# A transformer block on one core: another order of its pieces, three first loads through the Activation queue, multiplications by zero at the beginning, the last tile stored by halves

## The chip, the core and the metric

The kernel runs on one core of a Trainium2 chip. A core has a matrix engine (PE in the profile, with its weight loads shown as PEld), a vector engine (DVE), a scalar or activation engine (ACT), a general engine (POOL) and a synchronising engine (SP) that mostly issues DMA transfers. Each engine works through its own queue of instructions strictly in the order in which they were written and waits on semaphores for the others. The metric is the time of one launch in microseconds, as the device measures it; lower is better. The change is judged by the median of the runs.

## What is computed

One block of a transformer, all in float32: 2048 tokens of width 512, attention with 32 heads of width 16 in a sliding window of 256 tokens, and a gated feed-forward part of width 1376.

```python
h  = x + attention(layernorm(x), wqkv) @ wo      # causal, i - j < 256, softmax
g  = layernorm(h) @ w_gate                       # 512 x 1376
u  = layernorm(h) @ w_up                         # 512 x 1376
h2 = h + (sigmoid(g) * u) @ w_down               # 1376 x 512
```

## The kernel before

**Arithmetic.** Every float32 operand is split into a high and a low half of 16 bits, and a product is three matrix multiplications (high by high, high by low, low by high). So most of DVE's and ACT's work is to scale, to split (a cast for the high half, line 357 or 355, and a subtraction for the low one, line 362) and to take products out of PSUM. The weights need a scale first: the maximum of their absolute values (line 367 on ACT, line 369 on DVE), spread over the partitions by a small multiplication with the identity (line 380, the function `scale`).

**Tiles and stages.** The tokens are eight blocks `b` of 256, or sixteen tiles `t` of 128. For each block: layer norm (lines 556 to 573), split, transposition (the first four tiles by PE, line 609, the others by a DMA), query and key products (line 402, taken out at 661), a regrouping of queries and keys by DMA into `SQ` and `SK`, scores for the row maximum (lines 740 and 725), scores again in the transposed form (lines 794 to 805), exponentials on ACT (770), masks on POOL (778, 783), the product with V (831, taken out at 843), the division (873, 875), split into `whl`, and the product with `wo` (402 again, taken out at 899). The queries of a block go to `SQ` in transfers of 128 KB (`SQ<-sq`), the keys through DRAM (`mem<-sk`, then `SK<-mem`, 384 KB each).

The feed-forward part works on pairs of tiles `p` (0 to 7). Gate and up products are done in seven products instead of eight on operands that were added up beforehand (line 1140; the operands made of the weights come from lines 1026 and 1045, those made of the tokens from line 1122), the hidden values are gated and split (1206 to 1224), transposed by DMA (1240), and multiplied with `w_down` (function `do_down`, lines 1317 and 1323), whose weights are split at 954 and 956. `do_down` keeps two PSUM banks, A and B, of 512 columns; every half of a bank is a sum over many multiplications, and DVE adds it to the residual at lines 1288 and 1300. A finished tile of 128 by 512 is stored by line 1294 (256 KB).

**What sets the order.** Each step is a generator that yields, before each piece, what the piece needs and which engine it goes to. A planner has written down in which order the pieces are emitted: the table `ORDER` (lines 61 to 283), one number for each piece, which names the step and, where a piece can be done by more than one engine (`alt`: a cast on ACT or DVE, a subtraction on DVE or POOL), also the engine. `Planner.run` (line 312) replays it. The emitted order is the order of every engine's queue. PSUM has rings: three banks for the row maxima, two for transposed scores, two for the other products, and a single one for the product with V, so line 843 must have taken out one product before the next may start.

**The queue of the transfers.** Before the change all transfers are issued by SP, in one order. A transfer from SP waits until the one that held its semaphore eight transfers earlier is complete, and for the engines that its row names; everything behind it on SP waits too.

Of the kernel before, what the change touches and what calls it, by code (L numbers as in the profile page):

```python
# [35 lines left out]
P = 128  # L36
# [246 lines left out]
]  # L283

class Port(float):
# [1214 lines left out]
```

## Time and profile before

| | |
|---|---|
| runs | 770.92, 771.59 and 772.53 us, median 771.59 us |
| profiled execution | 770.99 us, of which its span (first to last instruction) is 769.3 us |
| mean granted clock of PE | 0.989 |
| busy in the span | PE 729.6, DVE 692.9, ACT 436.9, POOL 256.7 us |
| transfers | 118.57 MB, 154 GB/s on average |

Busy time counts an instruction from its start to its modelled end. A multiplication's end lies in the next ones, so a PE that is shown busy may still have short gaps. In the table of waits, each row names the instruction that waited, what released it, the sum of the waits, their number and the longest. In the windows, each engine's busy time in a stretch stands beside the granted clock of PE (1.00 is full speed), the mean busy share of the sixteen DMA engines and the GB/s they moved. In the list by time, a row is one instruction or a run of equal ones: start, duration, engine, line, operation, output and input.

### The profile page before, as it was taken

Reading aid. Unit: us, or ns where it says so; the run is one execution under the profiler, and the core shown is the slowest. Engines: PE = TensorE matmul, PEld = TensorE weight load, DVE = VectorE, ACT = ScalarE, POOL = GpSimd, SP = SyncE. Lnnn points to the kernel's source line nnn. Section 1 sums busy time; section 2 is a strip of 40 time slices with the busy share of each in tenths; the row PEclk is TensorE's granted clock in tenths of the full one; section 3 lists DMA queues with packets and bytes.
Section 4 is the critical chain, followed back from the end, with each engine's and each line's share of the span. In section 5 each row is a group of like instructions: output and inputs, shape, how many; then the busy total and the mean of one; then the engine's idle time right before and its main releaser. Section 6 shows DMA issues by size and latency. Waiting matters only on the chain.

```text
span 769.3 us, 19057 instructions
## 1 busy us (share of the span) xinstructions
PE 729.6 (95%) x7030; PEld 502.0 (65%) x7030; DVE 692.9 (90%) x2067; ACT 436.9 (57%) x774; POOL 256.7 (33%) x319
## 2 busy tenths in 40 slices
PE   4899999999999999999999898699999999999997
PEld 3586678777686687686666554367565666666476
DVE  8999999978899999999998579999998989989973
ACT  5755788878688888798877667653222111121210
POOL 3333445535545466554757442240000000000000
PEclk9999999999999999999999999899999999999999
DMA  8586593886747989569587879455375665736535
GB/s 300 156 221 168 142 180 80 152 198 144 165 95 172 205 211 182 166 156 245 150 162 180 211 187 274 117 119 105 79 136 95 117 131 106 150 66 109 96 83 155
DMA packets 210318, 118.57 MB, mean 154 GB/s; under 512 B 174576, under 2 KB 183792, under 8 KB 210224
## 3 DMA queue, kind: packets, MB, share of 16 engines
q1 hardware_dynamic: 210224, 117.35, 67.9%
q8 instruction: 55, 0.90, 0.5%
q14 instruction: 39, 0.32, 0.2%
HBM read 43.65 MB, written 19.40 MB: 82 GB/s over the span
## 4 chain that ended last, share of the span: by engine, by line
PE 75%; DVE 11%; DMA 5%; issue 5%; ACT 3%; SPq 0%; DVEq 0%; ACTq 0%
PE mmp L402 18%; PE sp L1140 14%; PE mmp L1317 11%; PE pvp L831 7%; PE sp L740 6%; PE stp L1140 6%; PE pvp L1140 3%; PE stp L805 2%; PE stp L795 2%; DVE junk L725 2%; PE stp L794 1%; PE mmp L1323 1%; PE stp L796 1%; DMA oT<-whl 1%; ACT pa L770 1%
## 5 line engine op out<-in xcount | busy, mean ns | idle before, releaser
L725 DVE CUSTOM_DVE_ANT_0 junk<-sp,mask 128x320 uint8<-128x320 f32 (+4 forms) x512 | 215.4, 465 | 16.6 <-PE sp L740 14.0
L770 ACT ACTIVATE pa<-stp,kappa 128x512 f32<-128x512 f32 (+1 forms) x256 | 157.3, 645 | 48.0 <-PE stp L796 44.5
L1140 PEld LDWEIGHTS <-x 128*128 128x128 f16 x1008 | 98.3, 98 | 94.6 <-issue 10.1
L740 PE MATMUL sp<-SK,SQ 96*128 96x256 f16 (+3 forms) x960 | 129.6, 233 | 6.3 <-DVE mq L725 3.1
L402 PE MATMUL mmp<-xT,W 128*128 128x256 f16 x768 | 114.3, 281 | 3.3 <-DVE sq L661 1.7
L740 PEld LDWEIGHTS <-SQ 96*128 96x128 f16 x960 | 80.5, 97 | 30.9 <-issue 12.8
L1140 PE MATMUL sp<-W,x 128*128 128x512 f16 (+1 forms) x420 | 90.1, 351 | 6.5 <-ACT SQ L355 5.8
L770 ACT ACTIVATE pb<-stp,kappa 128x512 f32<-128x512 f32 x128 | 84.6, 685 | 19.7 <-PE stp L805 15.9
L402 PEld LDWEIGHTS <-W 128*128 128x128 f16 x768 | 71.4, 100 | 16.1 <-DVE W L539 2.9
L778 POOL TENSOR_SCALAR_AFFINE_SELECT pa<-pa 128x1024 f32<-128x1024 f32 x56 | 62.9, 1127 | 53.9 <-ACT pa L770 50.3
L831 PE MATMUL pvp<-pa,VT 128*17 128x128 f32 (+1 forms) x1408 | 62.5, 307 | 0.0
L795 PE MATMUL stp<-SQ,SK 100*128 100x256 f16 x224 | 60.2, 272 | 0.0
L563 POOL TENSOR_TENSOR rs<-rs,nhalf 128x1 f32<-128x1 f32 x32 | 20.2, 634 | 118.2 <-DVE rs L560 105.0
L783 POOL TENSOR_SCALAR_AFFINE_SELECT pa<-pa 128x512 f32<-128x512 f32 x64 | 42.6, 669 | 45.3 <-ACT pa L770 45.0
L1206 ACT ACTIVATE SQ<-sp,cg 128x512 f32<-128x512 f32 (+1 forms) x22 | 14.0, 636 | 76.6 <-PE sp L1140 76.3
L796 PE MATMUL stp<-SQ,SK 100*128 100x128 f16 x256 | 55.5, 219 | 0.7 <-ACT pb L770 0.4
L783 POOL TENSOR_SCALAR_AFFINE_SELECT pb<-pb 128x512 f32<-128x512 f32 x64 | 42.0, 658 | 42.6 <-ACT pb L770 40.1
L402 PE MATMUL mmp<-WO,oT 128*128 128x512 f16 x192 | 51.4, 389 | 2.5 <-DMA oT<-whl 2.5
L831 PEld LDWEIGHTS pvp<-pa,VT 128*17 128x17 f32 x1408 | 37.8, 97 | 22.7 <-issue 2.7
L362 DVE TENSOR_TENSOR SQ<-SQ,SQ 128x512 f16<-128x512 f32 (+3 forms) x93 | 50.2, 555 | 1.9 <-ACT SQ L355 1.3
L794 PE MATMUL stp<-SQ,SK 100*128 100x128 f16 x224 | 49.5, 221 | 1.3 <-DMA SQ<-mt 0.3
L805 PE MATMUL stp<-SQ,SK 100*128 100x256 f16 x256 | 48.1, 272 | 2.5 <-ACT pa L770 2.1
(226 smaller groups left out, 1445.8 us busy)
## 6 DMA issues: line engine op xcount, KB each, us to landing
SQ<-sq SPq DMA_DIRECT2D x96, 128.0 KB
wr<-chunk SPq DMA_DIRECT2D x28, 256.0 KB
SK<-mem SPq DMA_DIRECT2D x16, 384.0 KB
chunk<-in_wd_dram SPq DMA_DIRECT2D x20, 256.0 KB
X<-in_x_dram SPq DMA_DIRECT2D x16, 256.0 KB
mem<-sk SPq DMA_DIRECT2D x8, 512.0 KB
out_dram<-X SPq DMA_DIRECT2D x16, 256.0 KB
W<-wr SPq DMA_DIRECT2D x7, 512.0 KB
```

What stands on the lines that cost most here:

```text
L402: PE.matmul(ps, a_of(a, k), b_of(b, k), start=(k == 0 and i == 0), stop=(k == n - 1 and i == 2))
L725: V.tensor_tensor_reduce(out=junk[:, c0:], in0=ps[:, c0:], in1=mask[:, c0:], scale=1.0, scalar=-3.0e38, op0=ALU.add, op1=ALU.max, accum_ou ...
L740: PE.matmul(ps[:, col:col + k1 - k0], q, SK[0:96, (2 * a + hf) % 5, 4 * (p % 2) + j, k0:k1], start=True, stop=True)
L770: S.activation(dst, a, AF.Exp, scale=kappa)
L778: G.affine_select(out=f, in_=f, pattern=[[0, 8], [-1, 128]], compare_op=ALU.is_gt, fill=0.0, base=0, channel_multiplier=1)
L783: G.affine_select(out=p, in_=p, pattern=[[0, 4], [1, 128]], compare_op=ALU.is_ge, fill=0.0, base=0, channel_multiplier=-1)
L795: PE.matmul(a[:, 128:384], ks(k0 + 1, g, j), qs(b, g, j, 0, 256), start=True, stop=True)
L796: PE.matmul(a[:, 384:512], ks(k0 + 3, g, j), qs(b, g, j, 128, 256), start=True, stop=True)
L805: PE.matmul(a[:, u, :], ks(k0 + 2, g, j + u), qs(b, g, j + u, 0, 256), start=True, stop=True)
L831: PE.matmul(ps[32 * j:32 * j + 17, u, q0:q1], VT[:, kt % 6, 8 * j + g, :], w[:, j, c:c + q1 - q0], start=first, stop=last, skip_group_chec ...
L1140: PE.matmul(ps, X2[p % 2][part][:, (a * COUNT[part] + at) * 2 + k, :], operand(c, j)[:, b, k, :], start=first and k == 0 and i == 0, stop= ...
L1317: PE.matmul(ps, hT[p, c, r][:, a, half * kinds[c] + i, :], W["d"][2 * c + i][:, b, j, :], start=fresh and c == 0 and i == 0 and n == 0, st ...
```

## The change

Four things are changed; all else in the program is the same.

1. The table `ORDER` is replaced as a whole. Its first row, before and after:

```diff
-    3203, 3331, 771, 899, 1027, 1155, 7424, 2179, 2435, 7808, 7426, 1411, 7424, 641, 2051, 7810, 7424, 641, 1539, 7424, 1667, 7808, 641, 7427, 7808,
...
+    3331, 899, 3203, 771, 1027, 1155, 7808, 3587, 2179, 7424, 2691, 2051, 7426, 641, 1539, 7810, 7424, 641, 2435, 7424, 7424, 641, 1795, 7808, 7427,
```

2. Tile 1 of x and the second and fourth quarter of the query weights are loaded by ACT's queue instead of SP's.

3. PE multiplies zeros: fourteen multiplications of 512 columns before anything else, two more behind the first group of eight transpositions and four behind the second. The operand is the buffer `stage[1][0]`, which POOL sets to zero at the beginning anyway; the result goes to a bank of the transposed scores and is not read.

4. In the last pair of tiles the last group of multiplications on bank A is emitted in another order. The three short multiplications that finish its upper 256 columns stand ahead of the last 15 + 3 on the lower ones; DVE then adds the upper half to the residual (line 1337 of the new file) and it is stored (line 1338); the lower half follows alone.

```diff
+    unread, zero = psum_tile("st", [P, 512]), stage[1][0].rearrange("p h j i u t -> p (h j i u t)")
+    turns = [2, 4]
+
+    def warm(n):
+        for i in range(n):
+            PE.matmul(unread, zero[:, :P], zero[:, :512], start=True, stop=True)
+
+    warm(14)
...
-        nc.sync.dma_start(xs[t][0], x[t * P:(t + 1) * P, :])
+        (nc.scalar if t == 1 else nc.sync).dma_start(xs[t][0], x[t * P:(t + 1) * P, :])
...
-        nc.sync.dma_start(wsrc[nm][:, k, :], src[k * P:(k + 1) * P, :])
+        (nc.scalar if nm == "q" and k % 2 else nc.sync).dma_start(wsrc[nm][:, k, :], src[k * P:(k + 1) * P, :])
...
+            if turns:
+                warm(turns.pop(0))
...
+            cols = slice(0, HALF if t == NT - 1 else D)
+            nc.sync.dma_start(out[t * P:(t + 1) * P, cols], home(t)[:, cols])
...
+                if ahead and c == 0:
+                    assert ("h", p, 2, ahead[0]) in plan.done
+                    rest(which, *ahead)
+                    x = home(2 * p + 1)[:, HALF:]
+                    V.scalar_tensor_tensor(x, bank[which][:, HALF:], cd, x, op0=ALU.mult, op1=ALU.add)
+                    nc.sync.dma_start(out[(2 * p + 1) * P:(2 * p + 2) * P, HALF:], x)
...
+        upper = 1, HALF, HALF, False
+        last = p == NT // 2 - 1
+        e = yield from step("A", 0, 5, 1, 1, False, [("r7", p)], ((1, 0, 0, False), upper), upper if last else None)
+        plan.add(prio, taken("r4", "A", t2, 0, HALF if last else D, [e, ("r7", p)], 0))
```

`rest` is the old loop over the short multiplications, now a function. The new file is 9 lines longer from line 446 on and up to 25 lines longer further down; in the rows below, lines 482 and 496 are the loads (473 and 487 before), 854 is 843, 886 is 875, 736 is 725, 697 is 686, 937 is 926 and 688 is 677.

**The start of ACT's queue.** Before, the loading of the table of functions stands first, and then the maxima of the query weights `wq` (each waits for a DMA semaphore) and their scaled copies:

```order
L1496 UNCONDITIONAL_BRANCH [waits barrier_Pool_Activation_PE_DVE_SP_release]
L367 ACT_TABLE_LOAD
L367 ACTIVATE W1_87,am_121<-wq_117 128x512 [waits DMAHW2_49]
L367 ACTIVATE W1_87,am_121<-wq_117 128x512 [waits DMAHW3_49]
L367 ACTIVATE W1_87,am_121<-wq_117 128x512 [waits DMAHW4_49]
L367 ACTIVATE W1_87,am_121<-wq_117 128x512 [waits DMAHW5_49]
L537 ACTIVATE W1_87<-wq_117,sq_196 128x512 [waits DVE_49]
```

After:

```order
L1521 UNCONDITIONAL_BRANCH [waits barrier_Pool_Activation_PE_DVE_SP_release]
L482 DMA X_69<-in_x_dram 128x512
L496 DMA wq_132<-in_wqkv_dram 128x512 x2
L367 ACT_TABLE_LOAD
L367 ACTIVATE W1_87,am_136<-wq_132 128x512 [waits DMAHW3_49]
L367 ACTIVATE W1_87,am_136<-wq_132 128x512 [waits DMAHW2_49]
L367 ACTIVATE W1_87,am_136<-wq_132 128x512 [waits DMAHW5_49]
L367 ACTIVATE W1_87,am_136<-wq_132 128x512 [waits DMAHW4_49]
L546 ACTIVATE W1_87<-wq_132,sq_204 128x512 [waits DVE_49]
```

Three transfers now stand ahead of the table's loading, and SP's queue has three fewer ahead of its next ones.

**SP's queue around one of the `SK<-mem` loads** (the keys of a block for the row maxima; in the execution before it is issued at 227.73 us). Before, rows 179 to 184 of SP's queue:

```order
L854 DMA_TRANSPOSE RT_75<-RH_77 128x8x128 [waits DMAHW7_49,DVE_49]
L752 DMA_TRANSPOSE mt_4154<-mh1_114 128x1x128 [waits DMAHW0_49,DVE_49]
L926 DMA chunk_4163<-in_wd_dram 128x512 [waits DMAHW1_49]
L756 DMA SQ1_79<-mt_4154 2x32x64 [waits DMAHW2_49,DMAHW0_49]
L756 DMA SQ1_79<-mt_4154 2x32x64 [waits DMAHW3_49]
L677 DMA SK_78<-mem_2887 96x2048 [waits DMAHW4_49,PE_49]
```

After, rows 179 to 184:

```order
L865 DMA_TRANSPOSE RT_75<-RH_77 128x8x128 [waits DMAHW6_49,Activation_49]
L767 DMA SQ1_79<-mt_4167 2x32x64 [waits DMAHW7_49,DMAHW5_49]
L767 DMA SQ1_79<-mt_4167 2x32x64 [waits DMAHW0_49]
L937 DMA chunk_4205<-in_wd_dram 96x512 [waits DMAHW1_49]
L937 DMA chunk_4220<-in_wd_dram 128x512 [waits DMAHW2_49]
L688 DMA SK_78<-mem_2918 96x2048 [waits DMAHW3_49,PE_49]
```

Two loads of the down weights (192 and 256 KB) stand directly ahead of the keys, where before there was one, with two small transfers between.

**DVE's queue ahead of one taking-out of a product with V** (the 26th of 32; in the execution before it is at 377.56 us). `whl` is the split of the attention's output, `rc` its reciprocal, `mh` the row maxima on their way to the queries. Before:

```order
L873 RECIPROCAL rc_7362<-OS_76 128x32 [waits Pool_49]
L357 CAST whl_7368<-OS_76 128x512 [waits DMAHW3_49,Pool_49]
L747 TENSOR_SCALAR mh0_113<-mq_6907 128x32 [waits DVE_49]
L748 SCALAR_TENSOR_TENSOR mh0_113<-mq_6907,mh0_113 128x32 [waits DVE_49]
L899 SCALAR_TENSOR_TENSOR X_69<-mmp_6940,co_2867,X_69 128x512
L362 TENSOR_TENSOR whl_7368<-OS_76,whl_7368 128x512
L843 SCALAR_TENSOR_TENSOR RH_77<-pvp0_111,RH_77 128x2x256 [waits Activation_49]
```

After:

```order
L736 ISA junk_7367,mq_6916<-sp_7350,mask_124 128x320 [waits DVE_49,PE_49]
L736 ISA mq_6916 128x1
L886 TENSOR_TENSOR OS_76<-OS_76,rc_6899 128x32x16
L854 SCALAR_TENSOR_TENSOR RH_77<-pvp0_126,RH_77 128x2x256 [waits Activation_49]
L736 ISA junk_7397,mq_7321<-sp_7386,mask_124 128x320 [waits DVE_49,PE_49]
```

The cast and the subtraction of this `whl` are no longer on DVE (they are on ACT and POOL), the row maxima's and the residual's rows come later, and a multiplication by an earlier reciprocal stands there instead.

More of the change, by code (lines that the diff above doesn't have):

```diff
@@ L1293, in taken @@
             e, = yield {DMA_: 0.475}, [e] + needs[1:], [], 0.73
-            nc.sync.dma_start(out[t * P:(t + 1) * P, :], home(t))
+            cols = slice(0, HALF if t == NT - 1 else D)
+            nc.sync.dma_start(out[t * P:(t + 1) * P, cols], home(t)[:, cols])
             plan.mark(("out", t), e)
@@ L1301, in high, with rest, step @@
             plan.mark((key, p), e)
-        def step(which, lo, j, r, half, fresh, needs, extra=()):
+        def rest(which, row, col, at, over):
+            R = F - (NF - 1) * P
+            for n, (a, b) in enumerate(((0, 0), (0, 1), (1, 0))):
+                PE.matmul(bank[which][:, at:at + HALF], hT[p, 2, row][:R, a, 2, :], W["l"][:R, b, col:col + HALF], start=over and n == 0, stop=n == 2,
+                          skip_group_check=not over)
+        def step(which, lo, j, r, half, fresh, needs, extra=(), ahead=None):
             nonlocal places
@@ L1318, in step @@
                                   stop=c == 2 and n == 2, skip_group_check=not fresh)
-            for row, col, at, over in extra:
-                e, = yield {PE_: 0.3265}, [("h", p, 2, row), ("W", "d", len(PAIRS))]
-                R = F - (NF - 1) * P
-                for n, (a, b) in enumerate(((0, 0), (0, 1), (1, 0))):
-                    PE.matmul(bank[which][:, at:at + HALF], hT[p, 2, row][:R, a, 2, :], W["l"][:R, b, col:col + HALF], start=over and n == 0, stop=n == 2,
-                              skip_group_check=not over)
+            for piece in extra:
+                e, = yield {PE_: 0.3265}, [("h", p, 2, piece[0]), ("W", "d", len(PAIRS))]
+                if piece != ahead:
+                    rest(which, *piece)
             return e
@@ L1338, in do_down @@
         plan.add(prio, taken("r3", "B", t1, 0, D, [e, ("r6", p)], 1))
-        e = yield from step("A", 0, 5, 1, 1, False, [("r7", p)], ((1, 0, 0, False), (1, HALF, HALF, False)))
+        upper = 1, HALF, HALF, False
+        last = p == NT // 2 - 1
+        e = yield from step("A", 0, 5, 1, 1, False, [("r7", p)], ((1, 0, 0, False), upper), upper if last else None)
         plan.mark(("hTf", p), e)
-        plan.add(prio, taken("r4", "A", t2, 0, D, [e, ("r7", p)], 0))
+        plan.add(prio, taken("r4", "A", t2, 0, HALF if last else D, [e, ("r7", p)], 0))
     work = kappa = cg = cd = hl2 = ws = None
```

440 rows, old and new, of the table ORDER are left out of this document.

## The prediction

> **What bounds the kernel now.** I read the page's totals first, then PE's waits, then windows, since a total hides which engine sets the pace where.
>
> ```profile
> span 769.3 us, 19057 instructions
> ...
> PE 729.6 (95%) x7030; PEld 502.0 (65%) x7030; DVE 692.9 (90%) x2067; ACT 436.9 (57%) x774; POOL 256.7 (33%) x319
> ```
>
> PE and DVE are both near full; ACT and POOL are not. PE's waits:
>
> ```profile
> PE mmp L609 <- DVE RT L357: 7.0, 1, 7.0
> PE sp L1140 <- ACT SQ L355: 6.4, 2, 5.8
> PE sp L740 <- DVE mq L725: 3.1, 6, 1.2
> PE mmp L402 <- DVE sq L661: 1.7, 1, 1.7
> PE sp L380 <- POOL RT L362: 1.6, 1, 1.6
> PE sp L740 <- DMA SK<-mem: 1.6, 1, 1.6
> PE mmp L1317 <- DMA RH<-SQ: 0.8, 1, 0.8
> ```
>
> They are the beginning (7.0, 1.6), one wait of 5.8 and one of 1.6 for keys. The windows show who is full around them (busy us by engine, PE's granted clock, DMA share, GB/s):
>
> ```profile
> core 0: us, PE busy (x) PEld busy (x) DVE busy (x) ACT busy (x) POOL busy (x), PEclk, DMA share, GB/s
> 0.00:12.30 12.30, 2.83 (x18) 2.01 (x18) 9.07 (x22) 4.83 (x11) 5.34 (x13) 1.00 0.84 270
> 22.00:24.00 2.00, 0.28 (x2) 0.10 (x3) 1.94 (x4) 1.98 (x5) 0.00 (x0) 1.00 0.17 66
> 26.00:28.00 2.00, 2.00 (x11) 1.40 (x10) 1.87 (x7) 1.22 (x2) 0.00 (x0) 0.50 1.03 170
> 12.30:138.00 125.70, 117.80 (x1209) 88.29 (x1210) 120.78 (x466) 92.52 (x187) 51.48 (x67) 0.99 0.67 168
> 138.00:200.00 62.00, 62.00 (x805) 47.32 (x802) 53.91 (x202) 49.67 (x86) 31.96 (x42) 1.00 0.75 162
> 204.00:212.00 8.00, 6.32 (x102) 4.34 (x101) 5.84 (x19) 3.72 (x7) 3.75 (x6) 1.00 1.05 217
> 212.00:216.00 4.00, 4.00 (x30) 3.25 (x30) 2.98 (x13) 2.63 (x4) 0.00 (x0) 0.57 0.56 171
> 344.00:392.00 48.00, 47.05 (x585) 32.11 (x588) 46.31 (x155) 40.02 (x67) 25.97 (x31) 1.00 0.81 190
> 452.00:484.00 32.00, 29.50 (x193) 13.93 (x193) 30.62 (x62) 23.50 (x42) 9.99 (x9) 0.95 0.97 240
> 484.00:496.00 12.00, 4.90 (x30) 2.82 (x29) 11.97 (x22) 7.37 (x15) 2.00 (x2) 0.85 0.50 120
> 496.00:500.00 4.00, 3.84 (x19) 2.11 (x18) 4.00 (x10) 2.51 (x6) 0.79 (x1) 0.60 0.42 93
> ```
>
> To 138 us DVE sets the pace (120.78 of 125.70; at 22 to 24 PE idles, and has half its clock at 26 to 28), then PE (62.00 of 62.00); at 344 to 392 both are full; at 452 to 496 DVE (30.62 and 11.97 of 44) makes PE idle, and PE then runs at 0.60.
>
> **The beginning.** The rows on which it turns:
>
> ```profile
> 0.94 1.81 POOL L444 MEMSET sq<- 128x2048 f32 x1
> 1.72 1.85 SPq L487 DMA_DIRECT2D wq<-in_wqkv_dram  x4
> 6.97 1.33 PE L609 MATMUL mmp<-identh,RT 128*128 128x128 f16 x8 [6.97 <-DVE RT L357]
> 6.45 0.63 ACT L367 ACTIVATE W<-wq 128x512 f16<-128x512 f32 x1 [4.37 <-DMA wq<-in_wqkv_dram]
> 8.85 0.63 ACT L367 ACTIVATE W<-wq 128x512 f16<-128x512 f32 x1
> 9.60 0.16 DVE L531 TENSOR_REDUCE am<-am 128x1 f32<-128x4 f32 x1 [1.05 <-ACT W L367]
> 9.91 0.76 PE L380 MATMUL sp<-ident,am 128*128 128x128 f32 x2 [1.60 <-POOL RT L362]
> 13.16 5.24 PE L402 MATMUL mmp<-xT,W 128*128 128x256 f16 x25 [0.18 <-DVE W L539]
> 18.24 0.39 PE L380 MATMUL sp<-ident,am 128*128 128x128 f32 x2
> 18.47 2.46 PE L402 MATMUL mmp<-xT,W 128*128 128x256 f16 x21
> ```
>
> The four `wq` quarters took SP 1.85 us to issue; by two queues the six first loads are issued about three issue times (1.4 us) sooner. What that is worth is bounded by DVE, which waited only 1.05 us for the last maximum: its rows ahead of that are its own work. Beside it, the small multiplication of `scale` took 0.76 us on a slow PE and 0.39 later. So at most 1.05 + 0.37 = 1.4 us come off. ACT now issues three transfers (0.46 each, 1.85 / 4) before loading its table, 1.4 us later; it idled 4.37 us ahead of its first quarter, so this is hidden, and would cost up to 1.4 only if that quarter came 3 us sooner.
>
> The Trainium skill ("Trainium Kernel Development and Optimization", Key Constraints) says that issuing from several engines saves only issue time, since the same 16 DMA engines move the data. By that the term is the 1.4 us of issue at most; the DMA share of 0.84 in the first window agrees.
>
> The fourteen zero multiplications start when POOL's memset ends, at 2.75. A column cost 210 ns / 256 at first (5.24 / 25) and 117 / 256 later (2.46 / 21), so 512 columns cost 0.42 or 0.23, and fourteen end at 8.6 (slow throughout) or 6.0. The transpositions were ready at 6.97. In the slow case they end at 9.9, the two zeros behind them (0.84) push `scale` from 9.91 to 10.8: a loss of 0.9. In the fast case nothing waits. I take −1.0, between −1.4 and +0.9. That faster PE makes the next products cheaper (25 × 93 ns = 2.3 us) I cost at nothing: from 12.3 us on DVE has its own 120.78 us to do. If DVE were not full there, this 2.3 would come on top.
>
> The Trainium skill ("TensorE: Matmul & The Clock Gate", What's actually happening) says that PE starts at half clock, is released after a busy window of about 3.4 us, and falls back after an idle one. The two prices per column agree, though the clock column reads 1.00 there. By the rule the zeros run slowly for some 3.4 us and end near 7.5, when the transpositions are 0.6 late and nobody waits for them: −1.0 as taken.
>
> **The order.** I counted DVE's rows up to each taking-out of a product with V (line 843; 32 of them), before and after, and priced each form by its mean:
>
> ```profile
> L369 DVE TENSOR_REDUCE amu<-chunk x7: 512/627/679, 124.3 to 199.1; 128x1 f32<-128x512 f32 x4, 128x1 f32<-128x352 f32 x3
> L369 DVE TENSOR_REDUCE amd<-chunk x7: 673/680/686, 196.1 to 247.2; 128x1 f32<-128x512 f32 x6, 96x1 f32<-96x512 f32 x1
> L362 DVE TENSOR_TENSOR whl<-OS,whl 128x512 f16<-128x512 f32 x9 | 6.6, 735 | 0.0
> L861 DVE TENSOR_TENSOR OS<-RT 128x272 f32<-128x272 f16 x17 | 8.5, 511 | 0.0
> ```
>
> DVE loses three `amd` (2.0), two `amu` (1.3) and two `whl` subtractions (1.5) and gains two additions at 861 (1.0); with the smaller moves its work up to the 32nd is 3.5 us less. ACT gets 2 and POOL 3 us more, which they have free. Up to the seventh (143.8 us) the work is equal: no gain where DVE is the bound. From 138 to 344 PE is full: no gain either. At 344 to 392 both are full, and there DVE's work up to the 26th taking-out is 4.8 us less but up to the 29th only 0.6 less: most of it is moved behind, not away. This frees the single PSUM bank sooner. The bounds are 0 (PE is the limit, idle 0.95 of 48) and 3 (DVE was, and all that is moved early counts); I take −1.5, nearer to what PE idles there. At 452 to 496 from DVE's last wait for PE to the first product's copy its rows are 1.0 us fewer, and PE waits for exactly that chain: −1.0, between −2.5 (the slow clock after it goes too: 0.40 × 4 = 1.6) and +1.5 (three `chunk` sums move from DVE to POOL, about 0.5 us slower each).
>
> **The end.**
>
> ```profile
> 760.20 0.48 DVE L1288 SCALAR_TENSOR_TENSOR X<-mmp,cd,X 128x256 f32<-128x256 f32 x1 [3.12 <-PE mmp L1317]
> 764.58 0.82 PE L1323 MATMUL mmp<-SQ,oT 96*128 96x256 f16 x6
> 765.44 0.75 DVE L1288 SCALAR_TENSOR_TENSOR X<-mmp,cd,X 128x512 f32<-128x512 f32 x1 [1.54 <-PE mmp L1323]
> ```
>
> The last DVE row shrinks from 0.75 to 0.48 (−0.27); the last store moves 128 instead of 256 KB, and from that row's end to the span's end it takes 3.1 us, of which the halving can save between 0 and 1.6; I take −0.3, nearer to 0, since the wait for its landing stays; the wait of 0.8 for `RH` goes, since its transposition now stands earlier on SP (−0.8). Against this the last 18 multiplications write the bank that line 1337 reads: PE drains, DVE takes 0.48, PE resumes: +0.75 with the handshakes. Behind the new store on SP stand the last two; its issue (about 0.5) lies beside 18 multiplications. Sum −0.6, cut to −0.5 since an operand's transposition (`WO`) now comes later; between −1.5 and +0.7.
>
> **Sum.** −1.0 − 1.5 − 1.0 − 0.5 = −4.0 us: the profiled execution's 770.99 would be 767.0. The median of the runs, 771.59, is 0.6 above that execution, so I forecast 767.6. All lower ends give −8.4, all upper ones +3.1.
>
> **Rivals.**
>
> ```profile
> 204.49 6.62 DMA SK<-mem
> ```
>
> *Keys come late twice (slower).* This load took 6.62 us behind 256 KB loads; PE waited 1.6 and then had a clock of 0.57 for 4 us (1.7 lost): 3.3. In the new order the next such load (before at 227.73, when nobody waited) has two loads of 448 KB together directly ahead; 192 KB more at 217 GB/s are 0.9. Price 4.2. PE then lets DVE catch up, so the −1.5 goes: −2.5 + 4.2 = +1.7, 773.3. It decides once that load takes over about 7 us of PE's work. Against it: it was not late before, with slack alike. Chance 0.17.
>
> *The late keys vanish.* A little less ahead of the load at 204.49 and its 3.3 us are gone: 764.3. Against it: two 256 KB loads still stand among the four rows ahead of it. Chance 0.15.
>
> *Nothing shows.* Zeros run slowly (+0.9), PE is the limit at 344 to 392 (0), the end is even: with the −1.0 left about 771.5. For it: PE idles only 0.95 in 48. Chance 0.14. The clock gate's rule leads here if the window falls badly.
>
> *My forecast*: 0.50; the last 0.04 lies outside all. The measurement tells 0.2%, 1.5 us, from no change. Faster: 0.50 + 0.15 + a little = 0.68; same 0.14; slower 0.18. The range takes in the late keys on one side and their absence with half of the lower ends on the other: 762.0 to 773.8; my forecast's own is 764 to 770.
>
> **What the new profile would show.** The wait at line 531 under 0.4 and `scale` at 0.39; zeros ended before 7.6; PE's idle at 22 to 24 us and the clock of 0.50 after it unchanged; PE's 5.8 wait about 1 shorter; a PE gap near 0.75 ahead of the last 18 multiplications and no wait for `RH`. I am wrong if a new wait for `SK<-mem` or `oT<-whl` over 1 us with a low clock behind it appears, or if DVE's window to 138 us shrinks by more than the start.

## The result, and the profile after

The changed kernel takes 773.99 us (median, 772.84 to 777.21), the kernel before, measured beside it, 769.74 us (765.75 to 772.53): the ratio is 1.0068, with a 95% interval of 1.0052 to 1.0085. It is slower by 4 to 5 us where 4 us less were forecast. The runs of the kernel before spread over 7 us here; so medians of several runs (4 to 30 of a kernel) are compared below, and a profile stands for one execution.

The page of the changed kernel's profiled execution (774.01 us):

```profile
span 772.3 us, 19120 instructions
...
PE 733.4 (95%) x7050; PEld 502.7 (65%) x7050; DVE 695.4 (90%) x2062; ACT 438.1 (57%) x782; POOL 257.3 (33%) x322
```

DVE is busy 2.5 us longer than before (692.9), though the order took work from it. That is the first sign of what happened. PE's waits after the change:

```profile
PE sp L1151 <- ACT SQ L355: 5.3, 2, 5.2
PE sp L751 <- DVE mq L736: 3.5, 5, 1.1
PE mmp L402 <- DVE sq L672: 3.2, 4, 1.5
PE stp L452 <- POOL sq L444: 2.8, 1, 2.8
PE mmp L402 <- DMA oT<-whl: 2.1, 2, 1.6
PE mmp L618 <- DVE whl L362: 1.8, 1, 1.8
PE sp L380 <- DVE am L540: 1.5, 2, 1.3
```

The 7.0 of the beginning is now 2.8 (the zero multiplications wait until POOL has set their operand to zero), the waits for `SK<-mem` (1.6) and for `RH` (0.8) are gone, and the other waits for DVE have grown. The same windows as before:

```profile
core 0: us, PE busy (x) PEld busy (x) DVE busy (x) ACT busy (x) POOL busy (x), PEclk, DMA share, GB/s
0.00:12.30 12.30, 8.52 (x38) 3.51 (x38) 8.87 (x22) 4.58 (x10) 5.41 (x13) 1.00 0.85 308
12.30:138.00 125.70, 113.73 (x1161) 85.74 (x1163) 119.48 (x451) 89.92 (x183) 49.30 (x63) 0.97 0.62 160
344.00:392.00 48.00, 46.70 (x585) 32.63 (x584) 45.23 (x153) 41.41 (x69) 24.78 (x32) 1.00 0.85 205
452.00:484.00 32.00, 26.45 (x183) 12.36 (x182) 31.01 (x58) 23.19 (x42) 7.83 (x8) 1.00 0.92 241
484.00:496.00 12.00, 8.06 (x45) 4.21 (x44) 12.00 (x23) 7.34 (x14) 3.23 (x3) 1.00 0.41 98
496.00:500.00 4.00, 1.68 (x6) 0.84 (x6) 3.96 (x7) 2.82 (x5) 0.51 (x1) 0.50 0.49 131
22.00:24.00 2.00, 0.49 (x4) 0.30 (x4) 1.94 (x4) 1.98 (x5) 0.00 (x0) 1.00 0.21 74
26.00:28.00 2.00, 2.00 (x11) 1.37 (x10) 1.87 (x8) 1.15 (x2) 0.00 (x0) 0.50 0.86 228
```

To 138 us PE does 4 us less work in the same time (113.73 against 117.80) while DVE is nearly full in both (119.48 and 120.78 of 125.70).

**Where the time goes.** The start of the same piece of PE's work in both profiled executions, taken from the lists by time, and its delay. Beside it stands a sum over DVE's rows up to there: what each row took beyond the usual time of its form. (The usual time is the lower quartile of the same line, operation and shape in the profiles compared; only rows more than 0.06 us above it count.)

| PE begins | before | after | delay | stretched DVE rows, after less before |
|---|---|---|---|---|
| first query product | 12.38 | 12.55 | +0.2 | 0.0 |
| first score | 42.83 | 44.20 | +1.4 | +1.4 |
| 30 scores on | 58.88 | 63.30 | +4.4 | +4.1 |
| first transposed score | 74.86 | 79.42 | +4.6 | +4.1 |
| 3rd product with V | 102.87 | 104.48 | +1.6 | +1.7 |
| 4th | 110.56 | 114.91 | +4.4 | +2.9 |
| 12th | 206.35 | 212.03 | +5.7 | +3.6 |
| 13th | 222.60 | 224.78 | +2.2 | +3.6 |
| 32nd | 452.04 | 453.61 | +1.6 | +5.3 |
| first `down` product | 497.32 | 500.03 | +2.7 | +6.8 |
| end of PE | 765.40 | 769.07 | +3.7 | +8.5 |
| end of the span | 769.28 | 772.29 | +3.0 | |

To the fourth product with V the delay rises and falls nearly with the stretched rows. Here are two of them, with what POOL did. First DVE, then POOL, in the changed kernel:

```profile
47.94 1.72 DVE L582 TENSOR_SCALAR xn<-X,mv,rs 128x512 f32<-128x512 f32 x1
59.14 2.02 DVE L582 TENSOR_SCALAR xn<-X,mv,rs 128x512 f32<-128x512 f32 x1
...
47.58 1.80 POOL L525 MEMSET SQ<- 32x2048 f32 x1
59.07 1.80 POOL L525 MEMSET SQ<- 32x2048 f32 x1
```

And the same row in the kernel before, away from such a setting:

```profile
47.56 0.55 DVE L573 TENSOR_SCALAR xn<-X,mv,rs 128x512 f32<-128x512 f32 x1
```

A row of 0.55 us took 1.72 and 2.02. It began while POOL set a part of `SQ` to zero, and ended 0.28 us after POOL did (47.58 + 1.80 = 49.38 against 49.66; 60.87 against 61.16). So it was held until POOL was through. All stretched rows are of this kind: in each of the seventeen profiles a POOL row ends inside every single one of them (29 of 29 before, 37 of 37 after), while this is so for 14 to 23% of the other rows. The Trainium skill ("SBUF — State Buffer", SBUF: two separate sides) says that DVE and POOL share one pair of SBUF ports under an exclusive lock: a DVE instruction in a two-port mode, or with two SBUF inputs against a POOL instruction that reads SBUF, and a POOL instruction exclude each other for the whole instruction. These rows agree: what they took beyond 0.55 (1.17 and 1.47) is the rest of POOL's row (1.44 and 1.73) less 0.27. The trace doesn't name a row's mode, but who was held, and beside what, fits the rule. The following counts are of the DVE rows in all seventeen profiles that began with 0.4 us or more of a POOL row still to run. None was held that read or wrote PSUM (0 of 3333); rows with two SBUF tensors as inputs were held beside POOL's masks, which read SBUF (147 of 148), and never beside its settings, which read nothing (0 of 57). POOL's rows are held by DVE's in their turn, but this doesn't tell the two orders apart (15.2 us of stretched POOL rows before, 13.2 after, counted in the same way).

### The profile page after: what moved, and what is told of

It is laid out like the page before. It is cut to its first block, busy times and chain, and to the rows that moved or that the text cites. A ratio compares the mean times of both kernels' runs of the same rounds, so it can differ in the third digit from the quotient of the medians.

```text
span 772.3 us, 19120 instructions
## 1 busy us (share of the span) xinstructions
PE 733.4 (95%) x7050; PEld 502.7 (65%) x7050; DVE 695.4 (90%) x2062; ACT 438.1 (57%) x782; POOL 257.3 (33%) x322
## 5 line engine op out<-in xcount | busy, mean ns | idle before, releaser
L736 DVE CUSTOM_DVE_ANT_0 junk<-sp,mask 128x320 uint8<-128x320 f32 (+3 forms) x512 | 214.4, 464 | 13.3 <-PE sp L751 10.5
L751 PE MATMUL sp<-SK,SQ 96*128 96x256 f16 (+3 forms) x960 | 131.6, 233 | 4.8 <-DVE mq L736 3.5
L402 PE MATMUL mmp<-xT,W 128*128 128x256 f16 x768 | 112.3, 276 | 6.1 <-DVE sq L672 3.2
L402 PEld LDWEIGHTS <-W 128*128 128x128 f16 x768 | 70.2, 98 | 19.5 <-DVE sq L672 4.0
L806 PE MATMUL stp<-SQ,SK 100*128 100x256 f16 x224 | 59.6, 271 | 0.0
L402 PE MATMUL mmp<-W,xT 128*128 128x512 f16 x192 | 49.6, 378 | 0.9 <-ACT VT L355 0.7
```

The costliest lines, as they stand in the source:

```text
L402: PE.matmul(ps, a_of(a, k), b_of(b, k), start=(k == 0 and i == 0), stop=(k == n - 1 and i == 2))
L736: V.tensor_tensor_reduce(out=junk[:, c0:], in0=ps[:, c0:], in1=mask[:, c0:], scale=1.0, scalar=-3.0e38, op0=ALU.add, op1=ALU.max, accum_ou ...
L751: PE.matmul(ps[:, col:col + k1 - k0], q, SK[0:96, (2 * a + hf) % 5, 4 * (p % 2) + j, k0:k1], start=True, stop=True)
L806: PE.matmul(a[:, 128:384], ks(k0 + 1, g, j), qs(b, g, j, 0, 256), start=True, stop=True)
```

## The experiments

The medians, and the stretched DVE rows of each profiled execution (all seventeen profiles form the quartiles). Each kernel was measured beside the kernel before on the same chip; that kernel's median lay between 768.86 and 769.74 us there. The ratio and its interval are worked out from all runs and aren't the quotient of two medians.

| kernel | median us | ratio to before (95%) | span of the profile | stretched DVE rows |
|---|---|---|---|---|
| before | 769.74 | | 769.3 | 12.4 |
| after | 773.99 | 1.0068 (1.0052 to 1.0085) | 772.3 | 21.0 |
| order_only | 776.82 | 1.0088 (1.0053 to 1.0123) | 776.5 | 21.2 |
| old_order | 768.40 | 0.9987 (0.9965 to 1.0009) | 768.3 | 12.5 |
| zeros_only | 768.56 | 0.9992 (0.9966 to 1.0017) | 767.3 | 12.2 |
| halves_only | 768.43 | 0.9991 (0.9965 to 1.0017) | 766.2 | 13.1 |
| after_split | 770.70 | 1.0021 (0.9999 to 1.0043) | 766.7 | 16.0 |
| before_split | 767.34 | 0.9978 (0.9958 to 0.9999) | 762.8 | 10.1 |
| new_to_5 | 776.04 | 1.0091 (1.0059 to 1.0123) | 775.8 | 17.1 |
| old_to_5 | 774.62 | 1.0082 (1.0055 to 1.0108) | 773.7 | 17.3 |
| new_seq_old_eng | 784.25 | 1.0186 (1.0163 to 1.0209) | 781.6 | 23.5 |
| old_seq_new_eng | 774.93 | 1.0064 (1.0044 to 1.0084) | 773.5 | 19.5 |
| keys_first | 766.96 | 0.9966 (0.9947 to 0.9984) | 765.4 | 11.9 |
| best2 | 765.27 | 0.9939 (0.9921 to 0.9956) | 763.2 | 11.1 |
| after_split_all | 767.97 | 0.9989 (0.9965 to 1.0013) | 766.2 | 13.5 |
| before_split_all | 765.71 | 0.9955 (0.9935 to 0.9975) | 763.1 | 10.5 |
| best3 | 767.54 | 0.9966 (0.9948 to 0.9984) | 766.4 | 11.3 |

### Which part of the change

**order_only** is the kernel before with the new table and nothing else:

```diff
 ORDER = [
-    3203, 3331, 771, 899, 1027, 1155, 7424, 2179, 2435, 7808, 7426, 1411, 7424, 641, 2051, 7810, 7424, 641, 1539, 7424, 1667, 7808, 641, 7427, 7808,
+    3331, 899, 3203, 771, 1027, 1155, 7808, 3587, 2179, 7424, 2691, 2051, 7426, 641, 1539, 7810, 7424, 641, 2435, 7424, 7424, 641, 1795, 7808, 7427,
...
```

> The kernel before with the new table ORDER and nothing else of the change. Theory A (the order itself costs: DVE's rows that PE needs between 33 and 63 us stand later in its queue): 4 to 5 us slower than before, with the first product for the scores at +1 to +2 us and the 30th score at about +4 us, as in the changed kernel. Theory B (the zeros and the loads on ACT's queue disturb the beginning, and the order only follows): within 1 us of before.

It took 776.82 us, ratio 1.0088. So the order alone costs about 7 us, at least as much as the whole change (the two intervals overlap): theory A, with a larger loss than its 4 to 5 us. The first score comes 2.3 us late (45.08 against 42.83) and the score 30 further on 5.3 us late.

**old_order** is the reverse, the changed kernel with the old table (the same diff with + and - exchanged):

> The changed kernel with the old table ORDER: loads on ACT's queue, zeros and the halves of the last tile remain. Theory A: 0 to 1.5 us faster than before (the halves are worth 0.5 to 0.7, the beginning about 0). Theory B: 3 to 5 us slower than before.

768.40 us, ratio 0.9987: the loads, the zeros and the halves together gain 0.6 us against the 769.01 beside them, and the interval includes no change.

**zeros_only** adds to the kernel before:

```diff
+    unread, zero = psum_tile("st", [P, 512]), stage[1][0].rearrange("p h j i u t -> p (h j i u t)")
+    turns = [2, 4]
...
+    warm(14)
...
+            if turns:
+                warm(turns.pop(0))
```

> The kernel before with the zero multiplications alone. Theory A: within 0.5 us of before, because DVE sets the pace from 12 us on; the first products of the queries start at 12.2 to 12.7 us as before. Theory B: 1 us or more slower.

768.56 us: no difference that can be seen, as theory A had it. The first query products began at 11.86 us, earlier than the 12.2 to 12.7 expected, and nothing came of it.

**halves_only** adds to the kernel before:

```diff
+        upper = 1, HALF, HALF, False
+        last = p == NT // 2 - 1
-        e = yield from step("A", 0, 5, 1, 1, False, [("r7", p)], ((1, 0, 0, False), (1, HALF, HALF, False)))
+        e = yield from step("A", 0, 5, 1, 1, False, [("r7", p)], ((1, 0, 0, False), upper), upper if last else None)
```

> The kernel before with the last tile stored in halves alone. Both theories: 0.3 to 0.8 us faster, since from PE's last product to the span's end the changed kernel takes 3.2 us instead of 3.9; if PE's gap ahead of the last 18 multiplications (about 0.75) eats it, the same.

768.43 us, 0.6 less than the 769.01 beside it, but the interval reaches over 1. The size is the expected one, but the runs don't show it.

### DVE's waits for POOL

**after_split** issues POOL's long settings in four pieces, with the same values in the same order of work; **before_split** does the same in the kernel before:

```diff
-        G.memset(SK[96:128, i].rearrange("r s t -> r (s t)").bitcast(F32), TWO)
+        for q in range(4):
+            G.memset(SK[96:128, i].rearrange("r s t -> r (s t)").bitcast(F32)[:, 256 * q:256 * q + 256], TWO)
...
-        G.memset(SQ[i][96:128, 8 * f:8 * f + 8].rearrange("r s i u t -> r (s i u t)").bitcast(F32), 0.0)
+        for q in range(4):
+            G.memset(SQ[i][96:128, 8 * f:8 * f + 8].rearrange("r s i u t -> r (s i u t)").bitcast(F32)[:, 512 * q:512 * q + 512], 0.0)
```

> The changed kernel with POOL's long settings of SK and SQ (0.95 and 1.80 us) issued as four pieces each, the same values in the same places. Theory P (DVE rows that begin while POOL works wait until POOL's row ends; the new order puts more of them there): the stretched DVE rows before 110 us (4.8 us in all up to the first transposed scores, and 1.3 at 105) shrink by 3 us or more, the first transposed scores come at 76 to 77 instead of 79.4 us, and the end 1 to 4 us earlier than the changed kernel (part of it goes into the wait for keys at 206 us). Theory D (the order alone: rows that PE needs stand later in DVE's queue): the same as the changed kernel within 0.5 us at 79 us and at the end.

> The kernel before with the same splitting alone. Theory P: the two stretches at 76 and 88 us (1.5 and 1.0) shrink, the second product with V comes 1 to 2 us earlier, and the end 0 to 1.5 us earlier. Theory D: no difference.

The changed kernel gains 3.3 us (773.99 to 770.70; ratio to before 1.0021), the kernel before 1.9 (0.9978). Nothing but the length of POOL's rows was changed; POOL does more work, and yet both are faster. The first transposed score comes at 76.0 us instead of 79.4, and the stretched rows up to there fall from 4.8 to 1.3 us. The first of the two rows shown above, and POOL's setting beside it, are now:

```profile
46.54 0.90 DVE L584 TENSOR_SCALAR xn<-X,mv,rs 128x512 f32<-128x512 f32 x1
...
46.18 2.19 POOL L527 MEMSET SQ<- 32x512 f32 x4
```

At the seventh product with V the early loss is gone: the two orders stand at 142.1 (new) and 142.3 us (old) with the settings in pieces, where 147.5 and 143.8 stood before. Profiles of the new table with long settings reach it at 147.5 (after) and 148.0 (order_only), those of the old table (before, old_order, zeros_only, halves_only) at 143.1 to 144.7. So what the changed kernel loses up to there hangs on POOL's long settings. The group of DVE's `xn` rows (twelve rows, the second number is their mean in ns) shows it, in the kernel before:

```profile
L573 DVE TENSOR_SCALAR xn<-X,mv,rs 128x512 f32<-128x512 f32 x12 | 7.6, 629 | 0.1
```

in the changed kernel:

```profile
L582 DVE TENSOR_SCALAR xn<-X,mv,rs 128x512 f32<-128x512 f32 x12 | 10.9, 905 | 0.8 <-POOL rs L572 0.8
```

in after_split:

```profile
L584 DVE TENSOR_SCALAR xn<-X,mv,rs 128x512 f32<-128x512 f32 x12 | 8.0, 670 | 1.4 <-POOL rs L574 1.4
```

and in before_split:

```profile
L575 DVE TENSOR_SCALAR xn<-X,mv,rs 128x512 f32<-128x512 f32 x12 | 6.8, 562 | 0.1
```

But 3.4 us remain between the two split kernels (770.70 against 767.34), with 16.0 against 10.1 us of stretched rows. So the remaining POOL rows (masks of 1024 columns, sums and subtractions of 256 and 512) were halved too, **after_split_all** and **before_split_all**:

```diff
+    def general(out, in0, in1, op):
+
+        if plan.on != POOL_:
+            V.tensor_tensor(out=out, in0=in0, in1=in1, op=op)
+            return
+        h = out.shape[1] // 2
+        for c in (slice(0, h), slice(h, 2 * h)):
+            G.tensor_tensor(out=out[:, c], in0=in0[:, c], in1=in1[:, c], op=op)
...
-            G.affine_select(out=f, in_=f, pattern=[[0, 8], [-1, 128]], compare_op=ALU.is_gt, fill=0.0, base=0, channel_multiplier=1)
+            for h in (f[:, 0:4], f[:, 4:8]):
+                G.affine_select(out=h, in_=h, pattern=[[0, 4], [-1, 128]], compare_op=ALU.is_gt, fill=0.0, base=0, channel_multiplier=1)
```

> As after_split, and every other long POOL row (the subtractions and sums of 256 or 512 columns, the masks of 1024) issued as two halves. Theory P (all that is left is the same waiting of DVE for POOL's longer rows): the sum of the stretched DVE rows falls from 16 us to under 12, and the kernel comes within 1.5 us of before_split_all. Theory D (the rest is the order of rows on DVE): the distance to before_split_all stays at 3 to 4 us.

> As before_split, with the same halves. Theory P: stretched rows from 10 us to 7 or less and 0 to 2 us faster than before_split (767.3). Theory D: 0 to 1 us slower, since POOL's rows take longer in two halves.

The changed kernel comes down to 767.97 us, the kernel before to 765.71. In all, shorter POOL rows are worth 6.0 us to the new order and about 3.5 (0.45% of 769) to the old one, though POOL is busy 26 us longer (283.1 against 257.3). The distance of the two orders shrinks from 4.3 to 3.4 to 2.3 us: theory P expected 1.5 at most, theory D 3 to 4. So about half of the loss is shown to go with the length of POOL's rows.

The other half stays open, and theory P doesn't carry most of it. The halves brought the stretched rows down to 13.5 us, not under 12, and left those of the old order as they were (10.1 and 10.5); its 1.6 us lie within the intervals. In the two profiles with all POOL rows shortened the new order is 0.2 us ahead at the seventh product with V, 1.5 behind at the twelfth and 2.1 behind at the last, of 3.1 at the span's end; the stretched rows up to these places differ by less than 0.8 us all the way. The largest step, 1.4 us, comes between the 16th and the 17th product, where PE waits 1.0 us for exponentials on ACT. Only the last 1.0 us, behind the last product, goes with more stretched rows (2.8).

### Sequence or choice of engine, first part or second

**new_to_5** and **old_to_5** splice the two tables behind the fifth product with V (121.91 us before); the rest of the other table follows without what is already done:

```python
pre = first[:cut]
done = Counter(code >> 2 for code in pre)
rest = [c for c in second if not (done[c >> 2] and not done.subtract([c >> 2]))]
ORDER = pre + rest
```

> The kernel before, its table taken from the new order up to the fifth product with V and from there the rest of the old one. Theory P: 4 us late at the fifth product with V, about 1 us late behind the wait for keys (which a late PE does not have), and 0 to 2 us slower than before at the end. Theory D: the same, so this run only tells where the time is lost: if more than 4 us are lost at the end, the first part of the order is to blame for all of it.

> The reverse: the old order up to the fifth product with V, then the rest of the new one. Theory P: on time at the fifth product, then DVE's stretched rows grow to 4 us more than before's by the end, and the kernel is 2 to 5 us slower. If it is within 1 us of before, the rest of the new order costs nothing.

776.04 and 774.62 us: both are slower, by 6.8 and 5.4 us, each as much as the whole change or more. New_to_5 is 4.7 us late at the fifth product against before and 6.6 late at PE's end: at the keys it wins back 2.2 (from +6.7 at the 12th product to +4.5 at the 13th), and between the 30th and the 31st it loses 2.2 again, where PE waits 2.5 us for exponentials on ACT. Old_to_5 is on time at the fifth (121.3), but from the 27th to the 28th product it loses 3.5 us against before, far behind the splice; PE waits 2.1 us there for the transfer `oT<-whl`, and no stretched row is added. The expectation that one half would be innocent fell: an order is not a sum of its parts, and what a splice costs needn't be DVE's waiting for POOL.

**new_seq_old_eng** and **old_seq_new_eng** keep one table's sequence and take from the other only which engine does a piece that has a choice (109 pieces of 4663 differ):

```python
engine = defaultdict(list)
for c in other: engine[c >> 2].append(c & 3)
ORDER = [c & ~3 | engine[c >> 2].pop(0) for c in ORDER]
```

> The changed kernel with the new sequence of pieces, but each piece that has a choice goes to the engine that the old table named. Theory S (the new sequence puts DVE's rows beside POOL's, above all POOL's long settings of SK and SQ): within 1.5 us of the changed kernel (774). Theory E (the new choice of engines, 3 us more on POOL, makes the collisions): 3 us or more faster than the changed kernel.

> The kernel before with the old sequence and the new choice of engines. Theory S: within 1.5 us of before (769). Theory E: 3 us or more slower. If DVE's 3.5 us of work less until the last product with V are worth something, as the prediction had it: 1 to 3 us faster.

784.25 and 774.93 us. Theory S fell in both runs, and theory E in the first, which is 10 us slower than the changed kernel where E expected it to be faster; only the second, 5.5 us slower than before, is as E had it. So sequence and choice fit each other, and neither can be exchanged alone. The stretched rows are 23.5 and 19.5 us. Old_seq_new_eng is slower by 0.64% although its DVE rows take 4.9 us less at their usual times (808.3 against 813.2): the work that the new choice saves didn't pay. That 7.1 us more of stretched rows are the reason fits, but this run doesn't show it alone.

Over all seventeen profiles the span grows with the stretched rows: the correlation is 0.91, and a fitted line gives 752 us plus 1.16 us for each stretched us. A correlation is no proof of a cause, and late rows also stand for other disorder; the split kernels are the experiment.

### The keys, and a version that beats both

**keys_first** moves two loads of weights (256 KB each) in the old order from ahead of one load of keys to behind it:

```diff
 ORDER = [
...
-    26896, 51715, 22531, 38912, 26883, 30083, 26883, 22541, 26627, 22531, 26900, 13187, 52739, 22545, 26904,
+    26896, 22531, 38912, 26883, 30083, 26883, 22541, 26627, 22531, 26900, 13187, 22545, 26904,
...
-    26908, 26883, 22557, 26627, 29699, 13187, 26912,
+    26908, 26883, 22557, 26627, 29699, 52739, 51715, 13187, 26912,
```

> The kernel before with two loads for the maxima of the feed-forward weights (256 KB each) moved in the order from ahead of one load of keys (issued at 204.49 us) to behind it. If the queue ahead makes that load late: PE's wait of 1.6 us and the low clock behind it go, and the end is 1.5 to 3 us earlier than before. If the load is slow whatever stands ahead: no difference.

766.96 us, ratio 0.9966. In the kernel before, SP issues the two loads and then the keys (with a transfer of queries between, left out here):

```profile
202.70 0.51 SPq L926 DMA_DIRECT2D chunk<-in_wu_dram  x1
...
203.87 0.52 SPq L926 DMA_DIRECT2D chunk<-in_wd_dram  x1
204.49 0.43 SPq L677 DMA_DIRECT2D SK<-mem  x1
```

Now it has the keys first:

```profile
202.59 0.52 SPq L651 DMA_DIRECT2D SK<-mem  x1
203.20 0.40 SPq L900 DMA_DIRECT2D chunk<-in_wd_dram  x1
203.70 0.38 SPq L900 DMA_DIRECT2D chunk<-in_wu_dram  x1
```

No wait of PE for `SK<-mem` is left in that profile, the stretch from the 12th to the 13th product takes 12.88 us instead of 16.26, and the median is 2.5 us lower. So the loads ahead made the keys late in the profiled execution of before. What this costs in other executions differs: of five more profiled kernels with the same table, two (zeros_only, old_order, where PE came 1.6 us later) show no such wait and also 12.88 us, and three (halves_only, before_split, before_split_all) a wait of 0.6 to 1.2 and 13.60 to 14.19 us. None of the five has the clock of 0.57 behind it. The 3.3 us at which the prediction had priced the late keys belong to that one execution; how much of the 2.5 us of the medians is theirs stays open.

**best2** puts together the old order with the keys first, the settings in four pieces, and the three small parts of the change; **best3** adds the halves of POOL's rows:

> The old order with the keys moved ahead as in keys_first, POOL's settings in four pieces, and the other three parts of the change (loads through ACT's queue, zeros, halves of the last tile). If the gains of the split (1.9), of the three parts together (0.6) and of the keys (1.5 to 3) add up: 764 to 766 us.

> best2 with the same halves of POOL's rows: 763.5 to 766 us by theory P, 765.3 or a little more by theory D.

765.27 us, ratio 0.9939 (0.9921 to 0.9956): faster than both kernels, by 4.2 us than before and 8.7 than after. The halves bring nothing on top: best3 takes 767.54 us, more than either theory expected, and its stretched rows stay as they are (11.3 against 11.1). Why they helped the other two kernels and not this one isn't shown.

## Why the prediction was wrong, point by point

**The step that failed is the order's price.** The prediction counted DVE's rows and "priced each form by its mean". The count was right in kind: at their usual times the changed kernel's DVE rows take 5.3 us less than before's (the sum of their durations less the stretched part, 807.9 against 813.2). But a DVE row has no fixed price here. The stretched part grew by 8.6 us (12.4 to 21.0), so DVE was busy 2.5 us longer. That waiting for POOL was in the trace of before, as a spread in the same rows (a mean of 629 ns for `xn`, where nine of twelve rows took 0.53 to 0.55 us and one 1.52), and I averaged over it. "ACT gets 2 and POOL 3 us more, which they have free" was wrong for POOL: its free time is not free for DVE. POOL was busy only 0.6 us longer (256.7 to 257.3), so it is not how much POOL does that counts, but beside which DVE rows it lies. About half of the loss is shown to hang on the length of POOL's rows; the cause of the other half stays open.

**"Up to the seventh (143.8 us) the work is equal: no gain where DVE is the bound."** Equal work took 3.7 us longer at the seventh product with V (143.81 against 147.52), with 2.8 us more of stretched rows.

**"From 138 to 344 PE is full: no gain either."** The delay went from +3.7 to +5.7 and back to +2.2 at the keys, which a late PE found ready though two loads stood directly ahead of them here too: the rival of the vanished keys came true, but for a reason that I had not named, and it returned less than had been lost. Part of it was luck of one execution, since the late keys of before, with their price of 3.3 us, are missing or cheaper in other profiles of the same table.

**344 to 392, −1.5**: from the 23rd to the 27th product the delay grew from +2.7 to +3.3, so +0.5. **452 to 496, −1.0**: from the 32nd product to the first `down` product +1.1 (1.57 to 2.71). The 5.8 wait for the copy on ACT went to 5.2, 0.6 shorter where about 1 was forecast, but the rows around it lost more. Two stretches had no term at all: from the 27th to the 32nd product 1.7 us came back, and from the first `down` product to PE's end another 1.0 was lost.

**The beginning, −1.0**: +0.2. These rows of the changed kernel answer to those shown of before:

```profile
2.81 5.68 PE L452 MATMUL stp<-sq 128*128 128x512 f16 x14 [2.81 <-POOL sq L444]
4.65 0.69 DVE L565 BATCH_NORM_STATS2 st<-X 128x6 f32<-128x512 f32 x1 [0.96 <-DMA X<-in_x_dram]
10.00 0.15 DVE L540 TENSOR_REDUCE am<-am 128x1 f32<-128x4 f32 x1
10.29 0.46 PE L380 MATMUL sp<-ident,am 128*128 128x128 f32 x2 [0.24 <-DVE am L540]
15.23 1.59 PE L402 MATMUL mmp<-xT,W 128*128 128x256 f16 x13 [0.16 <-DVE W L548]
```

The wait for the last maximum went and `scale` fell to 0.46 (0.39 was forecast), but DVE began its first row at 4.65 instead of 3.75, since it waited 0.96 us for the first tile of x. The loads on ACT's queue are the reason: in all seven profiles with them DVE began at 4.42 to 5.12, in all ten without at 3.59 to 3.82. That the six first loads, issued closer together, hold each other up is likely, but not shown. I had bounded the loss by the zeros alone. The fourteen zeros took 5.68 us (0.41 each) and ended at 8.49, not before 7.6 as forecast; nobody was late for them, because DVE's first rows were late as well; the products behind ran at 122 ns instead of 210 from the start, and this was worth nothing, as forecast, since DVE set the pace. PE's rest at 22 to 24 us and its half clock at 26 to 28 stayed, as forecast. By the rule of the Trainium skill ("TensorE: Matmul & The Clock Gate", What's actually happening), a release after a busy window of about 3.4 us, part of the zeros should have run at full clock: by the prediction's prices, eight at 0.42 us and six at 0.23 make 4.7 us. In three of the eight profiles with zeros the fourteen took 4.66 to 4.93 us, which agrees; in the other five, the changed kernel's 5.68 among them, they took up to 6.11, so there the slow price lasted longer.

**The end, −0.5**: −0.66 in the profiles (the delay falls from 3.67 at PE's end to 3.01 at the span's end), by the steps that were named:

```profile
766.41 0.48 DVE L1337 SCALAR_TENSOR_TENSOR X<-mmp,cd,X 128x256 f32<-128x256 f32 x1 [1.81 <-PE mmp L1318]
766.94 0.82 PE L1342 MATMUL mmp<-WD,RT 128*128 128x256 f16 x6 [0.57 <-DVE X L1337]
769.11 0.48 DVE L1299 SCALAR_TENSOR_TENSOR X<-mmp,cd,X 128x256 f32<-128x256 f32 x1 [1.56 <-PE mmp L1318]
```

PE's gap is 0.57, where 0.75 was taken. In medians it stays unresolved (halves_only 0.9991).

**The rivals.** Late keys at the load before at 227.73 did not occur: two loads directly ahead of it cost nothing. No rival and no sign of being wrong named a conflict between DVE and POOL, and my chance of 0.18 for slower rested on another mechanism: that its 773.3 lies near the measured 773.99 is chance.

## What to carry to other kernels

When an order is changed and DVE is near its limit, don't price DVE's rows by their means: look at the spread of each form, and at what POOL does during the long ones, for a long POOL row next to a DVE row that has all its tensors in SBUF can cost nearly its whole length. Cheap remedies come ahead of a new order: issue long POOL settings in pieces, and put a transfer that PE waits for ahead of bulk loads on the same queue; they gave 0.2 and 0.3% here, while a new order without them lost 0.7%. Half an order, or the choice of engines of one with the sequence of another, says little about the whole.

## What was not expected of the hardware

- A DVE row of 0.54 us took up to 2.0 us beside a POOL setting of 1.80 us on 32 partitions, and one of 0.17 us (the row maxima's `mh`, 32 columns) 1.6 us in the kernel before. What was held were rows with all their tensors in SBUF, never one that touched PSUM; with the settings cut in four, the two rows shown took 0.90 and 0.84.
- Splitting a POOL row cost little: four settings of a quarter took 2.19 us instead of 1.80, and halving everything raised POOL's busy time from 257.3 to 283.1 us, for a kernel 6.0 us faster.
- What stays open: 2.3 us between the two orders with all POOL rows shortened, most of it not DVE's waiting by the two profiles. It was not tried to take POOL out of a stretch altogether.
